# A gated-recurrence block and a bilinear FFN on one core: the output tile split by rows, and a unit's DMAs scheduled one by one

## The chip, the cores and the metric

The kernel runs on one core of a Trainium2 chip. The metric is the time of the whole program on the device, in microseconds: the median of several runs. Beside it there is one profiled execution, whose own time and span are given with the profile.

The core's engines run their own instruction lists in order and wait for each other on semaphores. They are named as in the profile: PE is TensorE (PEld its weight loads), DVE is VectorE, ACT is ScalarE, POOL is GpSimd, SP is SyncE, which does nothing here but put DMA transfers in (SPq in the rows). An instruction that must wait holds up all that is behind it on its engine.

## What is computed

```python
# attention: B, H, S, D = 4, 8, 768, 48
f = 1.0 / (1.0 + np.exp(-f_logit))
for t in range(S):
    state = f[:, :, t, :, None] * state + np.einsum('bhd,bhe->bhde', k[:, :, t], v[:, :, t])
    y[:, :, t] = np.einsum('bhd,bhde->bhe', q[:, :, t], state)
# bridge: (B, H, S, D) -> x of (B*S, H*D) = 3072 x 384
a = x @ w_a            # 384 x 1536
b = x @ w_b            # 384 x 1536
out = (a * b) @ w_out  # 1536 x 384
```

Everything is float32; the results have 3072 rows of 384.

## The kernel before

**Tiles and stages.** The 3072 tokens are cut into 8 blocks of 384 (half a sequence of one batch entry). A block's attention is done in two *units* of four heads each, 16 units in all. A unit is loaded into one of three sets of tiles (`NSET = 3`; `q`, `k`, `f`, `v`), so the loads of unit u + 3 can only follow when unit u is done.

A unit passes through these steps. The *front* (`front_parts`, L281): ScalarE makes two sigmoids of f (`opposite`, L294, and `sigmoid`, L291), GpSimd one affine step (L297), VectorE the running products (L301, L304, L309, L314), and multiplies q and k by them (L318). The *core* (`core_parts`, L845): TensorE makes scores of k and q (L364), VectorE masks them (L387), TensorE turns k (transposes, L399), ScalarE copies it out as `kT` (L409), TensorE forms the chunks' contributions to the state (`gains`, L423), VectorE adds them up (`carry`, L444 and L446, and `hand_on`, L455), TensorE forms y from the scores (`within`, L466) and from the state (`across`, L487), ScalarE copies y out of PSUM into `y_sb` (L512, three parts), and `stored` (L514) sends y into the block's `xT` by five DMAs (L531) and then issues the loads of unit u + 3: two of f, two of k and two of q (L215) and one of v (L217). `y_sb` has one buffer.

The FFN of a block is an *up*-projection (a, b and their product) and a *down*-projection. The first two blocks' ups are plain (`up`, L567). From the third block on the up is done with fewer products on sums of the operands (`combine_x`, L653, makes the sums with VectorE at L673; `up_triples`, L683, with matmuls at L689, copies by ScalarE and adds by VectorE, recorded at L1180 and L681). The down-projection takes token groups in pairs (`down`, L764, matmuls at L782), again with sums (L681). Each pair fills one tile `o` of 128 x 2 x 384, of which there is one buffer: row half 1 by `second` (ScalarE, L804), `sum_u3` (L813) and `last_of` (L816), row half 0 by `third` (ScalarE, L807) and `last_of`. `store(1)` and then `store(0)` send the halves out (SyncE, L820). `begin` copies one partial result to `u2` (L797).

**The order.** Startup, the weight conversions and the first four units are written out by hand. The rest is made by a list scheduler at build time. The list `main` holds the FFN's steps of the remaining blocks in order; each TensorE step is a *beat* of 656 ns. Every other step names its engine, an assumed load in ns and a `due`: the number of beats after which TensorE needs it. Beside `main` there are side lines (`Line`): sums of weights, sums of x, the core steps of the units, their fronts. `earliest` (L1099) gives the time at which a line's next step could start: the ends of the steps that it needs plus `LATENCY` (200 ns). `fill` (L1149) puts side steps in before each main step: a TensorE step when its inputs are ready by plan, another engine's step when its start is within a beat and `delays` (L1109) does not find that a due step of `main` on that engine would come late by it. `emit_until` (L1141) forces a line's steps in where main comes to need them (`beside`, `marks`).

In this plan the whole of `stored`, five stores and seven loads, is one SyncE step with a load of 0 ns, whose end is set 5000 ns after its start; the front of unit u + 3 needs that end. The output stores are SyncE steps of `main` with a load of 0 ns and no due.

Of the kernel before, what the change touches and what calls it, by code (L numbers as in the profile page):

```python
# [4 lines left out]

# [6 lines left out]
FP32 = mybir.dt.float32  # L12
# [9 lines left out]
BLK = 384  # L22
# [110 lines left out]
def by_quotients(ctx, tc, q, k, f_logit, v, moe_w_a, moe_w_b, moe_w_out, out, ident, weights, bad):  # L133
# [57 lines left out]
    def unit(u):  # L191
        b, r = divmod(u, NH * NQ)
        return (b, *divmod(r, NQ))

    def load_unit(u, names="fkqv"):
        if u >= NU:
            return
        b, half, qd = unit(u)
        t = sets[u % NSET]
        cols = slice(half * BLK, half * BLK + BLK)  # L200
        if u - NSET in FIRST and "f" in names:
            nc.gpsimd.memset(t["f"], 30.0)
        for nm, src in (("f", f_logit), ("k", k), ("q", q)):
            if nm not in names:
                continue
            if nm == "f" and u in FIRST:

                for par in range(2):
                    row = ((b * H + 4 * qd + par) * D) * S + half * BLK
                    rows = bass.AP(src.tensor, src.offset + row, [[S, R], [2 * D * S, 2], [1, BLK]])  # L210
                    nc.sync.dma_start(out=t[nm][R * par:R * par + R], in_=rows)
                continue
            heads = src[b].rearrange("(n two) d s -> two d n s", two=2)
            for par in range(2):
                nc.sync.dma_start(out=t[nm][R * par:R * par + D], in_=heads[par][:, 2 * qd:2 * qd + 2, cols])  # L215
        if "v" in names:
            nc.sync.dma_start(  # L217
                out=t["v"].rearrange("s n c x -> s n (c x)"),
                in_=v[b, 2 * qd:2 * qd + 2, :, half * NC:half * NC + NC].rearrange("n s c two d -> s n (c two d)"),
            )  # L220
# [293 lines left out]
    def stored(u):  # L514

        b, half, qd = unit(u)
        give_back(live[u].pop("y"))
        y = live[u].pop("y_sb").rearrange("r (n c) p m -> r n (c p m)", n=2)

        blk = b * NH + half  # L520
        if qd == 0:
            xT[blk] = sb2.tile([128, NKT, BLK], FP32, tag="xT", name="xT")
        for n in range(2):
            for h in range(2):
                ch, row, left = (4 * qd + 2 * n + h) * D, R * h, D
                while left:
                    kt, p = divmod(ch, 128)
                    w = min(left, 128 - p)

                    queue = nc.scalar if u < NQ and (n + h) % 2 else nc.sync  # L530
                    queue.dma_start(out=xT[blk][p:p + w, kt], in_=y[row:row + w, n])  # L531
                    ch, row, left = ch + w, row + w, left - w
        live.pop(u - NQ, None)
        if u >= NQ:
            load_unit(u + NSET)

# [5 lines left out]

    BEAT = 4 * 164
    beats = [0]

# [218 lines left out]
    def down(pair):  # L764
# [34 lines left out]
        def part(i, j):  # L799
            return got["o"][:, i, HM * j:HM * j + HM]  # L800

        def second():
            got["o"] = sb1.tile([128, 2, DM], FP32, tag="o", name="o")
            nc.scalar.copy(part(1, 0), m1)  # L804

        def third():
            nc.scalar.copy(part(0, 0), x0)  # L807

# [9 lines left out]
        def store(i):  # L818
            blk, g = pair[i]
            nc.sync.dma_start(out=out[blk * BLK + g * 128:blk * BLK + g * 128 + 128], in_=got["o"][:, i])  # L820

# [17 lines left out]
        yield on(DVE, 270, 8, last_of, 1, 0, x1)  # L839
        yield on(SP, 0, 0, store, 1)  # L840
        yield from times(m0, s4, b22)
        yield on(DVE, 270, 4, last_of, 0, 1, m0)
        yield on(SP, 0, 0, store, 0)

    def core_parts(s):  # L845
# [24 lines left out]
        if u >= 2 * NQ:  # L870
            for part in range(3):
                yield ACT, 490, 0, out_of_bank, u, part
            yield SP, 0, 5000, stored, u

# [33 lines left out]
    with tc.manual_schedule():  # L908
# [157 lines left out]

        for_out, for_x, core, fore, for_ba = lines = [Line() for _ in range(5)]
        marks = {"out": for_out.extend(w_out_sums)}
# [3 lines left out]
        for s in range(2 * NQ, NU + 1):  # L1072
            if s < NU:
                loaded = (stores[s - NSET],) if s - NSET in stores else ()
                ready = fore.extend(
                    [(e, load, 0, *do) for part in front_parts(s) for e, load, *do in part], needs=loaded
                )
            for step in core_parts(s):
# [5 lines left out]
                )  # L1084
                if step[3] is stored:
                    stores[s - 1] = core, len(core.steps)
            if s > 2 * NQ and s % NQ == 0:
# [21 lines left out]
        def delays(engine, start, load):  # L1109
# [11 lines left out]
            for ready, cost, due in later:  # L1121
                if ready >= with_it:
                    return False
                with_it, without = (max(x, ready) + cost for x in (with_it, without))
                if with_it + 2 * LATENCY > max(starts.get(due, 1 << 30), without + 2 * LATENCY):
                    return True
# [22 lines left out]
        def fill():  # L1149
            more = True  # L1150
            while more:
                more = False
                for line in lines:
# [4 lines left out]
                    if engine == PE:  # L1158
                        fits = start <= now
                    else:  # L1160
# [371 lines left out]
```

## Time and profile before

| what | value |
|---|---|
| median of 3 runs | 612.3 us (611.85 to 612.41) |
| the profiled execution's own time | 612.89 us |
| its span, first to last instruction | 610.6 us |
| mean granted TensorE clock | 0.977 |
| last matmul ends, last add on VectorE starts | about 604.3 us |

The stages of the span, in microseconds from its start:

| stage | from | to |
|---|---|---|
| startup, weight loads and conversions, plain ups | 0 | 126 |
| list scheduler begins; last plain ups, units 4 and 5 | 126 | 150 |
| three down pairs (with units 4, 5, 6 beside them) | 150 | 207 |
| first up with sums (third block) | 207 | 257 |
| one down pair, then ups and downs by turns, fronts and cores of later units beside them | 257 | 480 |
| ups and downs with no attention left | 480 | 604 |

Some more groups of the page, in their own columns: line, engine, operation, names, shape and count; then busy us and mean ns of one; then the idle time just before them and what ended most of it.

```profile
L689 PE MATMUL ps_f<-xT,w_ba 128*128 128x192 f32 x384 | 78.6, 327 | 0.8 <-ACT groups L1180 0.8
L782 PE MATMUL ps_f<-w_out,sums 128*128 128x192 f32 x288 | 51.6, 327 | 0.0
L297 POOL TENSOR_SCALAR inv<-inv 128x768 f32<-128x768 f32 x14 | 12.3, 881 | 258.4 <-ACT inv L294 258.3
...
out_dram<-o SPq DMA_DIRECT2D x24, 192.0 KB, 2.3
f_in<-in_f_logit_dram SPq DMA_DIRECT2D x28, 144.0 KB, 3.1
xT<-y SPq DMA_DIRECT2D x46, 72.0 KB, 2.2
```

The last three lines are DMA issues: what goes where, how many, KB of each, and the median us from issue to landing. How to read the rows: idle time before a group counts only on the engine that sets the end; on the others it is time in which they had nothing to do. A wait is put down to the event that came last before it ended, which need not be the one that was waited for.

### The profile page before, as it was taken

The page shows a single profiled execution, that of the slowest core. Times are in us where ns is not written, and L with a number is a line of the kernel's source. Part 1 is how long each engine was busy: PE and PEld are TensorE (multiplying, and loading weights), DVE is VectorE, ACT ScalarE, POOL GpSimd, SP SyncE. Part 2 cuts the span into 40 slices and gives each one's busy share as a digit, 9 for nine tenths or more (in the row PEclk, how much of TensorE's full clock was granted, in tenths as well). Part 3 has the DMA queues.
Part 4 walks back from the last instruction along what each step waited for, and adds up shares of the span by engine and source line. Part 5 has one row for each costly group of instructions (what it writes and reads, how often), then busy time and mean ns, then how long its engine had stood idle before and what let it go on. Part 6 is the DMA issues. An engine that isn't in the chain of part 4 may idle for free.

```text
span 610.6 us, 13870 instructions
## 1 busy us (share of the span) xinstructions
PE 572.2 (94%) x5778; PEld 512.7 (84%) x5778; DVE 409.4 (67%) x762; ACT 269.9 (44%) x508; POOL 75.1 (12%) x69
## 2 busy tenths in 40 slices
PE   0759899999989999999999999999999999999995
PEld 0625555556989989899999999999999999999995
DVE  6768434578978768968877875768576255836741
ACT  6567498962321554326532344335431245235300
POOL 6333164544200000000000100000000000000000
PEclk9859999999998999999999999999999999999998
DMA  8878586139855134044002600041001100000000
GB/s 221 251 204 232 143 259 206 53 66 163 154 125 124 47 84 93 2 103 119 1 3 74 149 27 1 2 109 36 1 3 47 46 0 1 1 27 0 2 28 31
DMA packets 33336, 49.42 MB, mean 81 GB/s; under 512 B 3952, under 2 KB 25072, under 8 KB 33264
## 3 DMA queue, kind: packets, MB, share of 16 engines
q1 hardware_dynamic: 29984, 42.38, 25.8%
q0 software_dynamic: 2992, 5.77, 5.6%
q8 instruction: 47, 0.77, 0.6%
q10 hardware_dynamic: 288, 0.30, 0.2%
q14 instruction: 25, 0.20, 0.1%
HBM read 33.23 MB, written 4.72 MB: 62 GB/s over the span
## 4 chain that ended last, share of the span: by engine, by line
PE 85%; DMA 6%; DVE 3%; ACT 2%; issue 2%; SPq 1%; ACTq 0%; DVEq 0%
PE ps_f L689 36%; PE ps_f L782 26%; PE ps_f L567 15%; DMA xT<-y 2%; PE ps_y L487 2%; PE ps_y L466 1%; PE ps_x L423 1%; PE ps_x L364 1%; DMA f_in<-in_f_logit_dram 1%; PE ps_x L399 1%; DMA k_in<-in_k_dram 1%; DVE sums L681 1%; DMA out_dram<-o 1%; SPq L215 1%; DMA q_in<-in_q_dram 1%
## 5 line engine op out<-in xcount | busy, mean ns | idle before, releaser
L567 PE MATMUL ps_f<-xT,w_ba 128*128 128x384 f32 x288 | 100.1, 506 | 6.9 <-DMA xT<-y 3.7
L567 PEld LDWEIGHTS ps_f<-xT,w_ba 128*128 128x128 f32 x288 | 55.1, 195 | 47.2 <-issue 7.4
L1180 ACT COPY groups<-ps_f 128x384 f32<-128x384 f32 x120 | 57.7, 481 | 66.6 <-PE ps_f L689 43.0
L1180 ACT COPY sums<-ps_f 128x384 f32<-128x384 f32 x120 | 57.6, 480 | 64.0 <-PE ps_f L689 56.6
L689 PE MATMUL ps_f<-xT,w_ba 128*128 128x192 f32 x384 | 78.6, 327 | 0.8 <-ACT groups L1180 0.8
L689 PEld LDWEIGHTS ps_f<-xT,w_ba 128*128 128x128 f32 x384 | 64.7, 190 | 1.5 <-ACT groups L1180 1.1
L689 PE MATMUL ps_f<-groups,w_ba 128*128 128x192 f32 x288 | 55.2, 327 | 0.0
L689 PE MATMUL ps_f<-x_sums,raw 128*128 128x192 f32 x288 | 53.8, 330 | 0.4 <-ACT sums L1180 0.2
L782 PE MATMUL ps_f<-spare,sums 128*128 128x192 f32 x288 | 51.7, 332 | 0.0
L782 PE MATMUL ps_f<-w_out,sums 128*128 128x192 f32 x288 | 51.6, 327 | 0.0
L782 PE MATMUL ps_f<-w_out,groups 128*128 128x192 f32 x288 | 51.2, 328 | 0.0
L689 PEld LDWEIGHTS ps_f<-x_sums,raw 128*128 128x128 f32 x288 | 47.1, 190 | 2.8 <-ACT sums L1180 1.7
L689 PEld LDWEIGHTS ps_f<-groups,w_ba 128*128 128x128 f32 x288 | 48.0, 190 | 0.4 <-ACT groups L1180 0.2
L782 PEld LDWEIGHTS ps_f<-spare,sums 128*128 128x128 f32 x288 | 47.4, 192 | 0.5
L782 PEld LDWEIGHTS ps_f<-w_out,groups 128*128 128x128 f32 x288 | 47.2, 190 | 0.6
L782 PEld LDWEIGHTS ps_f<-w_out,sums 128*128 128x128 f32 x288 | 47.2, 190 | 0.3
L59 POOL TENSOR_SCALAR sums<-sums 128x768 f32<-128x768 f32 (+1 forms) x20 | 40.4, 2019 | 51.4 <-ACT sums L57 51.4
L681 DVE TENSOR_TENSOR sums<-sums,groups 128x768 f32<-128x768 f32 x36 | 34.4, 955 | 14.8 <-ACT groups L1180 14.4
L297 POOL TENSOR_SCALAR inv<-inv 128x768 f32<-128x768 f32 x14 | 12.3, 881 | 258.4 <-ACT inv L294 258.3
L681 DVE TENSOR_TENSOR sums<-ps_f,sums 128x384 f32<-128x384 f32 x60 | 32.9, 554 | 13.9 <-PE ps_f L689 12.5
L689 PE MATMUL ps_f<-x_sums,w_ba 128*128 128x192 f32 x192 | 39.3, 327 | 0.2 <-DVE sums L681 0.2
L689 PE MATMUL ps_f<-xT,raw 128*128 128x192 f32 x192 | 39.3, 327 | 0.0
(123 smaller groups left out, 857.2 us busy)
## 6 DMA issues: line engine op xcount, KB each, us to landing
raw<-w_ba POOLq DMA_DIRECT2D x11, 512.0 KB, 8.2
q_in<-in_q_dram SPq DMA_DIRECT2D x32, 144.0 KB, 4.0
k_in<-in_k_dram SPq DMA_DIRECT2D x32, 144.0 KB, 3.5
v_in<-in_v_dram SPq DMA_DIRECT2D x16, 288.0 KB, 4.4
raw<-in_moe_w_out_dram SPq DMA_DIRECT2D x6, 768.0 KB, 4.2
out_dram<-o SPq DMA_DIRECT2D x24, 192.0 KB, 2.3
f_in<-in_f_logit_dram SPq DMA_DIRECT2D x28, 144.0 KB, 3.1
xT<-y SPq DMA_DIRECT2D x46, 72.0 KB, 2.2
```

The costliest lines, as they stand in the source:

```text
L59: nc.gpsimd.tensor_scalar(h, h, HI_MAX, None, ALU.min)
L215: nc.sync.dma_start(out=t[nm][R * par:R * par + D], in_=heads[par][:, 2 * qd:2 * qd + 2, cols])
L297: nc.gpsimd.tensor_scalar(inv, inv, EXP_K, 1.0, ALU.mult, ALU.add)
L364: nc.tensor.matmul(ps[h][SUB * p:SUB * p + SUB, o:o + SUB], lhsT=kf[r, tokens(n, c, p)], rhs=qf[r, tokens(n, c, p)], start=True, stop=True,)
L399: nc.tensor.transpose(ps[n][:, c * C:c * C + C], kf[:, o:o + C], ident)
L423: nc.tensor.matmul(ps_x[R * h:R * h + D, p, (n * NC + c) * D:(n * NC + c) * D + D], lhsT=kT[r, n, c, R * h:R * h + D], rhs=t["v"][r, n, c, ...
L487: nc.tensor.matmul(ps[p][e:e + D, o:o + SUB], lhsT=st[j][r, n], rhs=qf[r, tokens(n, c, p)], start=False, stop=True, skip_group_check=True,)
L567: nc.tensor.matmul(ps[nm][:, 0:BLK], lhsT=w[:, kt, ft * 128:ft * 128 + 128], rhs=xT[blk][:, kt], start=kt == 0, stop=kt == NKT - 1,)
L681: nc.vector.tensor_tensor(to, x, y, op)
L689: nc.tensor.matmul(ps[:, g], lhsT=sums_of_w[name][:, g, 128 * j:128 * j + 128], rhs=sums_of_x[blk][name], start=start and g == 0, stop=Tru ...
L782: nc.tensor.matmul(to, lhsT=x[:, i // 2, i % 2], rhs=w[:, NI * (i % 2) + i // 2], start=start and i == 0, stop=i == HFT - 1, skip_group_ch ...
L1180: do(*args)
```

## The change

It has three parts.

The output tile `o` becomes two tiles of 128 x 384, `o1` and `o0`, each with one buffer. `second` takes the first, `third` the other; `store(1)` reads the first and `store(0)` the other.

The DMAs of a unit become steps of their own for the list scheduler. `stores_of(u)` yields the bookkeeping (`begin`) and then each store of y, `loads_of(u)` each load. `core_parts` gives every store to the scheduler as a SyncE step of 430 ns (`ISSUE`) whose end is set 5000 ns behind it. A new side line, `loads`, holds the seven loads of the unit that takes the place of a stored one: each a SyncE step of 430 ns with an end 6000 ns behind it; the first needs the end of the last store, and the front of that unit needs the last load. The output stores become steps of 430 ns that are due after 3 beats, so that `delays` takes them into account. In the part written out by hand `stored` and `load_unit` run the same stores and loads in the same order as before.

The margins: `delays` allows 500 ns where it allowed 400 (`2 * LATENCY`), and a side step on TensorE is put in when its start by plan plus 200 ns (`LATENCY`) is not after the present, where it was its start alone.

```diff
     def load_unit(u, names="fkqv"):
+        for do in loads_of(u, names):
+            do()
+
+    def loads_of(u, names="fkqv"):
...
+        def load(to, src):
+            nc.sync.dma_start(out=to, in_=src)
...
             for par in range(2):
-                nc.sync.dma_start(out=t[nm][R * par:R * par + D], in_=heads[par][:, 2 * qd:2 * qd + 2, cols])
+                yield partial(load, t[nm][R * par:R * par + D], heads[par][:, 2 * qd:2 * qd + 2, cols])
...
     def stored(u):
 
+        for do in stores_of(u):
+            do()
+        if u >= NQ:
+            load_unit(u + NSET)
+
+    def stores_of(u):
+
         b, half, qd = unit(u)
-        give_back(live[u].pop("y"))
-        y = live[u].pop("y_sb").rearrange("r (n c) p m -> r n (c p m)", n=2)
-
         blk = b * NH + half
-        if qd == 0:
-            xT[blk] = sb2.tile([128, NKT, BLK], FP32, tag="xT", name="xT")
+
+        def begin():
+            give_back(live[u].pop("y"))
+            if qd == 0:
+                xT[blk] = sb2.tile([128, NKT, BLK], FP32, tag="xT", name="xT")
+            live.pop(u - NQ, None)
+
+        def store(n, h, kt, p, row, w):
+            y = live[u]["y_sb"].rearrange("r (n c) p m -> r n (c p m)", n=2)
+            queue = nc.scalar if u < NQ and (n + h) % 2 else nc.sync
+            queue.dma_start(out=xT[blk][p:p + w, kt], in_=y[row:row + w, n])
+
+        yield begin
         for n in range(2):
             for h in range(2):
                 ch, row, left = (4 * qd + 2 * n + h) * D, R * h, D
                 while left:
                     kt, p = divmod(ch, 128)
                     w = min(left, 128 - p)
-
-                    queue = nc.scalar if u < NQ and (n + h) % 2 else nc.sync
-                    queue.dma_start(out=xT[blk][p:p + w, kt], in_=y[row:row + w, n])
+                    yield partial(store, n, h, kt, p, row, w)
                     ch, row, left = ch + w, row + w, left - w
-        live.pop(u - NQ, None)
-        if u >= NQ:
-            load_unit(u + NSET)
...
     BEAT = 4 * 164
+    ISSUE = 430
...
         def part(i, j):
-            return got["o"][:, i, HM * j:HM * j + HM]
+            return got["o", i][:, HM * j:HM * j + HM]
 
         def second():
-            got["o"] = sb1.tile([128, 2, DM], FP32, tag="o", name="o")
+            got["o", 1] = sb1.tile([128, DM], FP32, tag="o1", name="o1")
             nc.scalar.copy(part(1, 0), m1)
 
         def third():
+            got["o", 0] = sb1.tile([128, DM], FP32, tag="o0", name="o0")
             nc.scalar.copy(part(0, 0), x0)
...
         yield on(DVE, 270, 8, last_of, 1, 0, x1)
-        yield on(SP, 0, 0, store, 1)
+        yield on(SP, ISSUE, 3, store, 1)
         yield from times(m0, s4, b22)
         yield on(DVE, 270, 4, last_of, 0, 1, m0)
-        yield on(SP, 0, 0, store, 0)
+        yield on(SP, ISSUE, 3, store, 0)
...
-            yield SP, 0, 5000, stored, u
+            begin, *stores = stores_of(u)
+            yield SP, 0, 0, begin
+            for do in stores:
+                yield SP, ISSUE, 5000, do
...
-        for_out, for_x, core, fore, for_ba = lines = [Line() for _ in range(5)]
+        for_out, for_x, core, fore, loads, for_ba = lines = [Line() for _ in range(6)]
...
-                loaded = (stores[s - NSET],) if s - NSET in stores else ()
+                loaded = ()
+                if s - NSET in stores:
+                    at = stores[s - NSET]
+                    loaded = (loads.extend([(SP, ISSUE, 6000, do) for do in loads_of(s)], needs=(at,)),)
...
-                if step[3] is stored:
-                    stores[s - 1] = core, len(core.steps)
+            if s > 2 * NQ:
+                stores[s - 1] = core, len(core.steps)
...
-                if with_it + 2 * LATENCY > max(starts.get(due, 1 << 30), without + 2 * LATENCY):
+                if with_it + 500 > max(starts.get(due, 1 << 30), without + 500):
...
-                        fits = start <= now
+                        fits = start + LATENCY <= now
```

## The prediction

> **What bounds the kernel now.** I read the page's first two parts first, to see which engine fills the span and where it does not.
>
> ```profile
> span 610.6 us, 13870 instructions
> PE 572.2 (94%) x5778; PEld 512.7 (84%) x5778; DVE 409.4 (67%) x762; ACT 269.9 (44%) x508; POOL 75.1 (12%) x69
> ...
> PE   0759899999989999999999999999999999999995
> ...
> PEclk9859999999998999999999999999999999999998
> ```
>
> TensorE sets the time: 572.2 of 610.6 us, and after the first six slices it is full but for slices 12 and 13. So only what makes TensorE wait, or slows its clock, can move the end. The profiled execution took 612.89 us, 2.3 us more than its span; the median of the runs is 612.3, so its stalls are taken as those of the runs and subtracted from 612.3.
>
> Next the windows of 15 us, for TensorE's missing time and its clock. Up to about 126 us (the last weight conversions) the order is written out by hand, and the change issues the same things in the same order there. From 315 to 600 us TensorE is busy 285.00 of 285.00 us: nothing can be won there. Between them stand the rows that matter (columns: length, then busy time of PE, PEld, DVE, ACT, POOL with counts, clock, DMA share, GB/s):
>
> ```profile
> 165.00:180.00 15.00, 14.67 (x178) 14.06 (x176) 12.51 (x23) 1.42 (x4) 0.00 (x0) 1.00 0.54 127
> 180.00:195.00 15.00, 13.16 (x142) 13.09 (x143) 11.97 (x29) 3.53 (x9) 0.83 (x1) 0.89 0.52 124
> ...
> 210.00:225.00 15.00, 14.18 (x261) 13.32 (x260) 9.37 (x16) 7.10 (x15) 0.83 (x1) 1.00 0.44 101
> 225.00:240.00 15.00, 14.96 (x90) 14.00 (x89) 13.69 (x28) 8.41 (x19) 0.00 (x0) 1.00 0.45 99
> 240.00:255.00 15.00, 14.57 (x174) 13.29 (x173) 12.87 (x25) 7.75 (x15) 0.83 (x1) 1.00 0.01 2
> ...
> 285.00:300.00 15.00, 14.10 (x173) 13.26 (x172) 11.88 (x18) 8.22 (x17) 0.83 (x1) 1.00 0.29 68
> 300.00:315.00 15.00, 14.82 (x92) 14.53 (x91) 11.84 (x19) 7.08 (x17) 0.00 (x0) 1.00 0.01 1
> ```
>
> The missing time is 0.33 + 1.84 = 2.17 us around 180, 0.82 us in 210 to 225, and 0.04 + 0.43 + 0.90 + 0.18 = 1.55 us after it: 4.54 us in all. The clock of 0.89 in 180 to 195 costs more: a finer window, 183.2 to 186.6, shows 0.50, so 3.4 us of matmuls did 1.7 us of work. The most that the change can win is thus 4.54 + 1.7 = 6.2 us, one per cent.
>
> Then the timeline, for what ended those waits. The first, in order of time (SPq is SyncE issuing a DMA):
>
> ```profile
> 167.27 0.37 SPq L820 DMA_DIRECT2D out_dram<-o  x1
> 167.73 3.04 SPq L531 DMA_DIRECT2D xT<-y  x5
> ...
> 173.83 0.42 SPq L217 DMA_DIRECT2D v_in<-in_v_dram  x1
> 174.34 0.42 SPq L820 DMA_DIRECT2D out_dram<-o  x1
> ...
> 178.90 0.32 ACT L804 COPY o<-ps_f 128x192 f32<-128x192 f32 x1 [8.43 <-DMA out_dram<-o]
> ...
> 180.99 0.80 ACT L409 COPY kT<-ps_x 128x768 f32<-128x768 f32 x1
> ...
> 181.84 0.70 PE L423 MATMUL ps_x<-v_in,kT 64*48 64x48 f32 x38 [2.16 <-ACT kT L409]
> ```
>
> The second output half of the pair was summed by 168.56 (its add on VectorE starts at 168.20 and takes 0.36), but its store stands in SyncE's order behind five stores and seven loads of an attention unit and goes out at 174.34. The next pair writes into the same single buffer `o`; ScalarE therefore stood 8.43 us, and behind it stood the copy of kT that TensorE needs. Its transposes were done at about 178.4, so kT could have been there before 179.7, where TensorE ran dry.
>
> The second wait: ScalarE's L294 for the front of unit 9 starts at 216.86 after 3.87 us idle. The view names an add on VectorE that does not write its inputs; the second load of f_in was issued at 213.8 and such loads land after 2.8 to 3.6 us, which is 216.6 to 217.4. So this is a front put before its data had come; L1180 behind it was late and TensorE lost 0.82 us.
>
> **The output tile as two.** No instruction is added or removed: 24 stores of 192 KB, 24 copies and 48 adds of `o` stay. `second` now waits for store 1 of the pair before (issued 167.27, landing 1.8 to 4.8 us later, so by 172.1) and would be ready at about 172.1 (its matmuls run from 169.95 to 171.9). `third` waits for store 0, and is ready at about 174.0; with the store out at 168.6 it lands by 170.4 to 173.4. What stands behind `second` on ScalarE is L294, `third`, L291 and the kT copy at L409; TensorE waits for the last. All 2.17 us go if store 0 is not held up; if it is, `third` waits instead and the copy behind it with it. The two waits of ScalarE on that tile are 12.3 us; the other one, 3.9 us ending at 195.89, costs TensorE nothing (15.00 of 15.00 us busy from 195 to 210) and I count it at nothing.
>
> The slow clock followed at 183.2, that is 3.5 us after TensorE ran dry at 179.7, and TensorE was at full speed in every other window from 60 to 600 us, with waits of up to 0.9 us from 185 on. So I put it down to this gap and take all 1.7 us; from below the bound is 0. The Trainium skill, "TensorE: Matmul & The Clock Gate", section "HAM oscillation — how this bites in real kernels", speaks against that: by it only idle gaps of more than about 3.4 us matter, and 2.17 us would not drop the clock. By that rule the sum would be 1.7 us smaller, 609.3; the row shows the drop after the shorter gap, and I go by the row.
>
> **DMAs one by one, loads behind the stores.** The 5 stores and 7 loads of a unit remain 12 issues on SyncE, 3.04 us and about 3.2 us in the timeline. Now each is a step of 430 ns, an output store can go between them, and the loads follow only when the last store is 5.2 us past by plan. For unit 4 (y copied out by 164.9) stores end by plan at about 167.3 and loads start at 172.5: store 0 of the pair (168.6) is ahead of them. The front of the unit three later is planned 5 x 0.43 + 5.2 + 7 x 0.43 + 6.2 = 16.6 us after the first store, where it was 5.2. The real way is 3.4 us of stores, 1.8 us for the two f_in issues and 3.0 us of landing, 8.2 us: the old plan was too early and the new one is not. The 0.82 us of the second wait go; bounds 0 to 0.82, and I take 0.82 because nothing else in ScalarE's queue was late there.
>
> Cost of the delay of 11.4 us per unit: unit 7 was stored from 227.4, and the sums of its block (L673) start at 257.1, after the up-projection before them has ended; 239 would still be 18 us ahead of them. Unit 5, the tight one, was stored at 184.3, its sums ran from 193.5 to 199.1 and their use began at 207.3, 8.2 us of cover; its stores come earlier by up to 2.6 us (kT at 178.4 instead of 181.0), and the plan pays 2.2 us more for five issues. Hence nothing. Without that cover each us late would be a us of TensorE.
>
> **Wider margins.** Side work on VectorE and ScalarE is refused 100 ns sooner, and a side step on TensorE is put in 200 ns after its inputs' planned end. The steps stay the same; each may slip by a beat (0.65 us), hidden by the same slack. This is aimed at such waits as the 0.90 us at 293.9 (transposes for a mask not yet done) and four of about 0.2 us. No row shows how the new order falls out. Bounds: it wins all 1.55 us, or adds as much again. I take 0, the middle, since VectorE is 13.69 of 15 us busy at 225 to 240, where any new order is as exposed as the old.
>
> **Sum.** 2.17 + 1.7 + 0.82 + 0 = 4.7 us; 612.3 - 4.7 = 607.6. All terms at their best give 606.1; without the second wait and with 1.55 us added, 2.17 + 1.7 - 1.55 = 2.3 gives 610.0.
>
> **Rivals.** (a) Only the first stall goes, the second stays and the new order adds small ones of 1.55 us: 610.0 by the sum above. For it: such waits come from plans that differ from the chip by a few hundred ns, and 100 ns more margin is less than the 0.9 us seen. Against: the front no longer meets its loads.
>
> (b) A ScalarE queue blocked elsewhere takes the place of the first: fronts wait for k_in on VectorE six times, 9.8 us in all, up to 3.5 us, with TensorE's copies behind them. One gap like the first, with its slow clock, is 3.9 us: 607.6 + 3.9 = 611.5, no measurable change. Against: none of those six reached TensorE with more than 0.9 us.
>
> (c) Slower: the fronts, now 10 us later, pile up on VectorE in the first up-projection in threes (207 to 257). A front is 2 x 0.95 + 0.15 + 0.17 + 6 x 0.43 + 2 x 0.95 = 6.7 us of VectorE. The front of unit 9 moves from 217 to about 227 and would meet that of unit 10 (240 to 257) where VectorE has only 1.31 + 2.13 = 3.4 us free in 225 to 255. If it is put in all the same, 6.7 - 3.4 = 3.3 us of adds come late and TensorE waits as long, and the front of the next unit does it again: two such waits, each with the clock at half for 1.7 us, are 10 us, 607.6 + 10 = 617.6. It decides when new stalls exceed 4.7 + 1.2 = 5.9 us. Against: work that would make a due add late is refused by plan, more so than before, and unit 7 has 18 us of cover.
>
> **How the numbers follow.** A measurement of this kernel can tell 0.2%, 1.2 us, from no change. Chances: the forecast 0.62, (a) 0.12, (b) 0.10, (c) 0.16. Faster is the first two, 0.74; same is (b), 0.10; slower is (c), 0.16. The forecast's own range is 606.0 to 609.5. The range that should hold 8 in 10 runs from 605.7 (all terms at best, and 0.4 us for the two lengths of wait that I could not see) to 612.8, past (a) and (b), and leaves out most of (c).
>
> **What would show it.** Right: ScalarE's wait for the landing of `out_dram<-o` is gone from its waits; the output store of 174.34 stands ahead of the unit's loads; the clock is 1.00 in every window from 75 to 600; TensorE's missing time from 165 to 315 falls from 4.5 to under 2 us; the f_in load is issued well before L294 asks for it. Wrong: a new wait of over 1 us of TensorE in 165 to 350, on VectorE for (c), on ScalarE for (b); or a clock of half without a gap, which would take the 1.7 us out of the sum. A change of the time before 126 us or after 600 us would mean that something else than these steps moved it.

## The result, and the profile after

The changed kernel takes 611.91 us (median of 12 runs, 611.11 to 612.98), the kernel before 612.04 us (12 runs). The ratio is 0.9995, its 95% interval 0.9984 to 1.0007: no change that can be measured. The line numbers below are those of the changed kernel: matmuls of the plain ups L588, of the ups with sums L710, of the downs L803; adds L702; copies L1208; the front L301 to L328; `second` L825, `third` L829; kT L419; output stores L842.

The page of the changed kernel, its span and the granted clock in 40 slices:

```profile
span 611.1 us, 13867 instructions
...
PEclk9859999999999999999999999999999999999998
```

The slice of slow clock near 185 us is gone, as forecast, yet the span is not shorter. The windows of 15 us show where the time went (length, then busy time of PE, PEld, DVE, ACT, POOL with counts, clock, DMA share, GB/s):

```profile
165.00:180.00 15.00, 15.00 (x237) 14.61 (x227) 12.97 (x26) 2.74 (x7) 0.00 (x0) 1.00 0.51 134
180.00:195.00 15.00, 15.00 (x165) 14.70 (x164) 11.06 (x25) 4.70 (x10) 0.83 (x1) 1.00 0.47 119
...
210.00:225.00 15.00, 15.00 (x205) 14.49 (x197) 12.64 (x26) 6.50 (x14) 0.00 (x0) 1.00 0.46 101
225.00:240.00 15.00, 14.71 (x180) 14.06 (x179) 11.01 (x24) 9.15 (x20) 0.83 (x1) 1.00 0.13 36
240.00:255.00 15.00, 14.42 (x174) 13.83 (x173) 14.79 (x24) 5.93 (x14) 0.83 (x1) 1.00 0.35 67
255.00:285.00 30.00, 29.79 (x422) 28.47 (x421) 21.35 (x49) 12.90 (x28) 0.83 (x1) 1.00 0.25 69
285.00:300.00 15.00, 14.79 (x91) 14.48 (x90) 12.90 (x23) 7.46 (x15) 0.00 (x0) 1.00 0.38 90
300.00:315.00 15.00, 13.80 (x180) 11.97 (x181) 13.07 (x24) 6.83 (x15) 0.83 (x1) 1.00 0.01 1
315.00:600.00 285.00, 283.16 (x2550) 276.29 (x2543) 179.72 (x320) 99.79 (x220) 2.50 (x3) 1.00 0.11 30
```

The same long window of the kernel before:

```profile
315.00:600.00 285.00, 285.00 (x2573) 280.05 (x2572) 180.25 (x323) 101.82 (x222) 2.50 (x3) 1.00 0.11 30
```

The two early waits are gone (15.00 of 15.00 us from 165 to 225). But from 225 on TensorE misses time in every row, and 1.84 us in the long window where it had missed none.

A wait costs more than its idle time: some of the matmuls after it are slower too, by about 0.1 us each (at 370.05 us of the changed kernel, right after a wait, the next one starts 0.27 us later; the usual distance there is 0.16). So I went through TensorE's list, matmul by matmul, took the distance from one start to the next, less the usual distance between two matmuls of these two kinds (the median), and summed what exceeded it by over 0.05 us, stage by stage. The expectations quoted below count only pauses of over 0.11 us, which gives smaller numbers (1.85 for 2.90, 1.17 for 2.05). "Scheduled" is the time from the second matmul that the list scheduler placed (near 129 us) to the end of the last one; it leaves out the startup, which varies (last section). All in us:

| stage | before | after |
|---|---|---|
| three downs, 150 to 207 before | 4.98 | 0.66 |
| up of block 2 | 3.58 | 2.39 |
| up of block 3 | 2.36 | 3.79 |
| up of block 4 | 0.29 | 2.90 |
| up of block 5 | 0.51 | 2.05 |
| all else | 3.06 | 2.77 |
| sum | 14.78 | 14.56 |
| scheduled | 474.95 | 474.74 |

The changed kernel wins 4.3 + 1.2 + 0.3 = 5.8 us and loses 1.4 + 2.6 + 1.5 = 5.6 us. The table accounts for the whole difference (14.78 - 14.56 = 0.22, 474.95 - 474.74 = 0.21).

What is won, in the timeline of the changed kernel (start, duration, engine, line, what, idle time before it):

```profile
167.18 2.35 SPq L842 DMA_DIRECT2D out_dram<-o  x2
169.62 3.04 SPq L545 DMA_DIRECT2D xT<-y  x5
172.64 0.32 ACT L825 COPY o<-ps_f 128x192 f32<-128x192 f32 x1 [1.63 <-PE ps_f L803]
174.59 0.32 ACT L829 COPY o<-ps_f 128x192 f32<-128x192 f32 x1 [1.63 <-DVE w_ba L1167]
179.64 0.80 ACT L419 COPY kT<-ps_x 128x768 f32<-128x768 f32 x1 [4.73 <-DVE o L835]
181.44 0.70 PE L433 MATMUL ps_x<-v_in,kT 64*48 64x48 f32 x38
184.47 0.94 ACT L304 ACTIVATE inv<-f_in,less 128x768 f32<-128x768 f32 x1
```

Both output stores go out before the unit's stores, and ScalarE waits for TensorE and not for a landing (for L829 and L419 the view names work on VectorE that they do not read; the matmuls that they read ended at 174.55 and 179.56). TensorE takes kT without idle time. But note the last row: the front of unit 7 (L304) now stands behind the copy of kT, where it stood ahead of it before (179.11 against 180.99). That turns out to matter.

What is lost, at the worst place in the up of block 4:

```profile
368.38 0.47 DVE L324 TENSOR_TENSOR_SCAN inv<-inv,start,zero 128x128 f32<-128x128 f32 x1
368.77 0.40 DVE L324 TENSOR_TENSOR_SCAN inv<-inv,zero 128x128 f32<-128x128 f32 x1
369.08 0.46 DVE L324 TENSOR_TENSOR_SCAN inv<-inv,start,zero 128x128 f32<-128x128 f32 x1
369.46 1.00 DVE L702 TENSOR_TENSOR groups<-ps_f,groups 128x384 f32<-128x384 f32 x2
370.05 2.22 PE L710 MATMUL ps_f<-x_sums,raw 128*128 128x192 f32 x12 [0.90 <-DVE groups L702]
```

VectorE works on the front of unit 14 (L324), the two adds that free TensorE's PSUM banks (the memory that the matmuls write) come after it, and TensorE stands 0.90 us. The same place in the kernel before:

```profile
356.31 0.95 DVE L318 TENSOR_TENSOR k_in<-k_in,inv 128x768 f32<-128x768 f32 x1
370.61 1.14 DVE L681 TENSOR_TENSOR groups<-ps_f,groups 128x384 f32<-128x384 f32 x2 [0.54 <-PE ps_f L689]
371.64 2.11 PE L689 MATMUL ps_f<-x_sums,raw 128*128 128x192 f32 x12
```

There the front's last step (L318) was long done, and VectorE waited for TensorE. In the kernel before this front began at 347.2 (its L294), in the down-projection ahead, and ended at 357.3, 4 us into this up; now it runs from 358.6 to 376.7, deep inside it. That of unit 15 ran from 409.2 to 421.6, to 10 us into the up of block 5, and now from 418.1 to 436.0, to 27 us into it.

### The profile page after: what moved, and what is told of

Read it like the earlier page. It is cut to its first block, busy times and chain, and to the rows that moved or that the text cites. A ratio compares the mean times of both kernels' runs of the same rounds, so it can differ in the third digit from the quotient of the medians.

```text
span 611.1 us, 13867 instructions
## 1 busy us (share of the span) xinstructions
PE 572.6 (94%) x5778; PEld 511.6 (84%) x5778; DVE 410.5 (67%) x762; ACT 268.7 (44%) x508; POOL 76.1 (12%) x69
## 4 chain that ended last, share of the span: by engine, by line
PE 82%; DVE 5%; DMA 5%; ACT 2%; issue 2%; SPq 1%; ACTq 0%; DVEq 0%
PE ps_f L710 32%; PE ps_f L803 27%; PE ps_f L588 15%; DMA xT<-y 2%; PE ps_y L476 2%; PE ps_y L497 2%; PE ps_x L433 2%; PE ps_x L374 1%; DVE groups L702 1%; PE ps_x L409 1%; DMA f_in<-in_f_logit_dram 1%; DVE sums L702 1%; DMA k_in<-in_k_dram 1%; DVE inv L324 1%; DVE f_in L311 1%
## 5 line engine op out<-in xcount | busy, mean ns | idle before, releaser
L588 PE MATMUL ps_f<-xT,w_ba 128*128 128x384 f32 x288 | 99.6, 505 | 7.0 <-DMA xT<-y 3.7
L588 PEld LDWEIGHTS ps_f<-xT,w_ba 128*128 128x128 f32 x288 | 55.1, 195 | 47.0 <-issue 7.4
L1208 ACT COPY sums<-ps_f 128x384 f32<-128x384 f32 x120 | 57.6, 481 | 75.3 <-PE ps_f L710 68.7
L1208 ACT COPY groups<-ps_f 128x384 f32<-128x384 f32 x120 | 57.7, 481 | 68.4 <-PE ps_f L710 47.8
L710 PE MATMUL ps_f<-xT,w_ba 128*128 128x192 f32 x384 | 78.5, 327 | 0.0
L710 PEld LDWEIGHTS ps_f<-xT,w_ba 128*128 128x128 f32 x384 | 64.7, 190 | 0.3
L710 PE MATMUL ps_f<-x_sums,raw 128*128 128x192 f32 x288 | 53.7, 330 | 2.6 <-DVE groups L702 2.0
L710 PE MATMUL ps_f<-groups,w_ba 128*128 128x192 f32 x288 | 55.6, 328 | 0.0
L710 PEld LDWEIGHTS ps_f<-x_sums,raw 128*128 128x128 f32 x288 | 47.0, 190 | 5.5 <-DVE groups L702 3.2
L803 PE MATMUL ps_f<-w_out,groups 128*128 128x192 f32 x288 | 51.6, 328 | 0.0
L803 PE MATMUL ps_f<-w_out,sums 128*128 128x192 f32 x288 | 51.5, 327 | 0.0
L803 PE MATMUL ps_f<-spare,sums 128*128 128x192 f32 x288 | 49.8, 327 | 0.0
L710 PEld LDWEIGHTS ps_f<-groups,w_ba 128*128 128x128 f32 x288 | 47.9, 190 | 0.8 <-ACT sums L1208 0.4
L803 PEld LDWEIGHTS ps_f<-w_out,groups 128*128 128x128 f32 x288 | 47.2, 190 | 0.6
L803 PEld LDWEIGHTS ps_f<-w_out,sums 128*128 128x128 f32 x288 | 47.4, 190 | 0.2
L702 DVE TENSOR_TENSOR sums<-sums,groups 128x768 f32<-128x768 f32 x36 | 35.3, 980 | 18.0 <-ACT groups L1208 17.6
L803 PEld LDWEIGHTS ps_f<-spare,sums 128*128 128x128 f32 x288 | 47.0, 190 | 0.1
L702 DVE TENSOR_TENSOR sums<-ps_f,sums 128x384 f32<-128x384 f32 x60 | 33.0, 553 | 20.0 <-PE ps_f L710 16.2
L710 PE MATMUL ps_f<-x_sums,w_ba 128*128 128x192 f32 x192 | 39.6, 329 | 1.0 <-DVE groups L702 0.5
L710 PE MATMUL ps_f<-xT,raw 128*128 128x192 f32 x192 | 39.8, 330 | 0.2 <-ACT groups L1208 0.2
```

The costliest lines, as they stand in the source:

```text
L588: nc.tensor.matmul(ps[nm][:, 0:BLK], lhsT=w[:, kt, ft * 128:ft * 128 + 128], rhs=xT[blk][:, kt], start=kt == 0, stop=kt == NKT - 1,)
L702: nc.vector.tensor_tensor(to, x, y, op)
L710: nc.tensor.matmul(ps[:, g], lhsT=sums_of_w[name][:, g, 128 * j:128 * j + 128], rhs=sums_of_x[blk][name], start=start and g == 0, stop=Tru ...
L803: nc.tensor.matmul(to, lhsT=x[:, i // 2, i % 2], rhs=w[:, NI * (i % 2) + i // 2], start=start and i == 0, stop=i == HFT - 1, skip_group_ch ...
L1208: do(*args)
```

## The experiments

Two theories of the give-back: **A**, the planned ends of the new DMA steps (16.6 us from a unit's first store to the front three units later, where it was 5.2) push the fronts into the ups with sums; **B**, something else does, the margins above all. Ratios are to runs of the kernel before on the same chip, with 95% intervals.

| experiment | ratio | interval | scheduled | downs to 207 | up 2 | up 3 | up 4 | up 5 |
|---|---|---|---|---|---|---|---|---|
| before | 1 | | 474.95 | 4.98 | 3.58 | 2.36 | 0.29 | 0.51 |
| after | 0.9995 | 0.9984 to 1.0007 | 474.74 | 0.66 | 2.39 | 3.79 | 2.90 | 2.05 |
| tile only | 0.9972 | 0.9947 to 0.9998 | 471.55 | 2.19 | 3.02 | 2.36 | 0.29 | 0.51 |
| old margins | 1.0006 | 0.9980 to 1.0032 | 474.92 | 1.09 | 2.86 | 1.80 | 2.89 | 2.05 |
| margins only | 0.9966 | 0.9944 to 0.9988 | 473.27 | 1.64 | 5.87 | 1.47 | 0.29 | 0.98 |
| one tile | 0.9987 | 0.9965 to 1.0009 | 474.46 | 0.66 | 2.39 | 3.79 | 2.63 | 2.04 |
| fronts held | 0.9948 | 0.9929 to 0.9967 | 472.44 | 0.66 | 2.38 | 3.79 | 0.46 | 0.74 |
| real loads | 0.9924 | 0.9902 to 0.9947 | 471.54 | 1.09 | 4.20 | 1.46 | 0.59 | 1.24 |
| one step, real end | 0.9938 | 0.9913 to 0.9962 | 471.84 | 0.83 | 1.69 | 3.51 | 0.53 | 0.74 |
| plan's wait alone | 0.9983 | 0.9960 to 1.0005 | 473.38 | 1.18 | 2.92 | 1.80 | 1.27 | 1.89 |
| slower issues | 0.9950 | 0.9933 to 0.9967 | 472.08 | 0.83 | 2.14 | 2.55 | 1.32 | 2.59 |
| tile and margins | 0.9965 | 0.9948 to 0.9983 | 474.01 | 1.93 | 6.31 | 1.47 | 0.29 | 0.98 |

### Old margins: are they the cause?

The changed kernel with these two lines as before:

```diff
-                if with_it + 500 > max(starts.get(due, 1 << 30), without + 500):
+                if with_it + 2 * LATENCY > max(starts.get(due, 1 << 30), without + 2 * LATENCY):
...
-                        fits = start + LATENCY <= now
+                        fits = start <= now
```

> The changed kernel with the old margins (400 ns, and TensorE's side steps without the 200 ns). Theory A (what the change wins early it gives back because the loads' planned ends put the fronts of later units 11 us later, into the ups with sums): the fronts of units 14 and 15 stay in the ups of blocks 4 and 5, as the plan has them, and the new waits of about 3.7 us there stay: 611.2 to 612.6 us. Rival B (the wider margins moved the side work): these waits go and the early gain is kept: about 608.0 us.

The run took 611.89 us. The ups of blocks 4 and 5 lose 2.89 and 2.05 us, as in the changed kernel (2.90 and 2.05). The margins are not what gives the gain back there; with the other two parts of the change in place they are worth 474.92 - 474.74 = 0.2 us. That is a sum of larger parts: without them the up of block 3 loses 1.80 us instead of 3.79, but the down-projection before it 1.58 instead of 0.33, and the first downs and the up of block 2 lose 0.43 and 0.47 us more.

### Margins only

The same two lines changed in the kernel before, and nothing else.

> The kernel before with the wider margins alone; one output tile, a unit's DMAs in one step. Theory A: ScalarE still stands for the landing of the output half near 179 and the clock drops after it, so the early 3.9 us are not won; the fronts of units 14 and 15 stay where they were and the ups of blocks 4 and 5 have no new waits: 611 to 612.5 us. Rival B (margins cause the give-back): the early loss stays and about 4 us of new waits come to it: about 616 us.

609.65 us. The ups of blocks 4 and 5 keep their pace (0.29 and 0.98), so theory B fails a second time. But my expectation failed too: the early wait is gone, without the tile or the new DMA steps. The wider margins changed the order of SyncE's work, so that both output stores go out ahead of the unit's DMAs (L807 is `third`, and it waits for TensorE):

```profile
164.05 2.35 SPq L820 DMA_DIRECT2D out_dram<-o  x2
166.50 3.04 SPq L531 DMA_DIRECT2D xT<-y  x5
171.47 0.32 ACT L807 COPY o<-ps_f 128x192 f32<-128x192 f32 x1 [1.63 <-PE ps_f L782]
```

The up of block 2 pays for part of it with 5.87 us: the fronts there now come before their f_in data, and ScalarE waits for such loads for 8.7 us in all between 165 and 225.

### Tile only

The kernel before with `o1` and `o0` and nothing else.

```diff
...
-            got["o"] = sb1.tile([128, 2, DM], FP32, tag="o", name="o")
+            got["o", 1] = sb1.tile([128, DM], FP32, tag="o1", name="o1")
...
+            got["o", 0] = sb1.tile([128, DM], FP32, tag="o0", name="o0")
...
```

> The kernel before with the output tile split in two and nothing else: SyncE's order of DMAs and all margins stay. Theory A (the queue holds the stall, the tile alone frees little): the store of row half 0 still goes out behind five stores and seven loads at about 174.3 and lands at about 178.9; now `third` waits for it instead of `second`, and L294 and `second` get ahead. The copy of kT stands behind `third`, so TensorE's gap near 181 shrinks by at most 1 us and the clock still drops: 611 to 612 us. Rival B (the single tile is the cause, its split is enough): the gap of 2.17 us and the slow clock of 1.7 us go: 608.1 us.

611.43 us, ratio 0.9972. The median lies in A's range, but the interval is wide (0.1 to 3.2 us won); in the profile the scheduled part is 3.4 us shorter, more than A says and less than B. The timeline of this kernel (L808 is `third`):

```profile
174.07 0.94 ACT L294 ACTIVATE inv<-f_in,less 128x768 f32<-128x768 f32 x1 [2.18 <-DMA f_in<-in_f_logit_dram]
...
178.23 0.32 ACT L808 COPY o<-ps_f 128x192 f32<-128x192 f32 x1 [3.13 <-DMA out_dram<-o]
178.44 0.85 ACT L291 ACTIVATE f_in<-f_in 128x768 f32<-128x768 f32 x1
179.19 0.79 ACT L409 COPY kT<-ps_x 128x768 f32<-128x768 f32 x1
...
180.03 0.70 PE L423 MATMUL ps_x<-v_in,kT 64*48 64x48 f32 x38 [0.89 <-ACT kT L409]
```

The mechanism is A's: the landing is now waited for by `third`, with the kT copy behind it. But L294 has already run, and the copy comes at 179.19 instead of 180.99 (1.16 us earlier in the scheduled part, which began 0.64 us earlier here); TensorE's gap is 0.89 instead of 2.16 us, and the clock stays at full speed. So in the three downs the split alone wins 2.8 of the 4.3 us: a gap shorter by 1.27 us, and no slow clock after it.

### One tile

The changed kernel with the single tile `o`.

```diff
...
-            got["o", 1] = sb1.tile([128, DM], FP32, tag="o1", name="o1")
+            got["o"] = sb1.tile([128, 2, DM], FP32, tag="o", name="o")
...
-            got["o", 0] = sb1.tile([128, DM], FP32, tag="o0", name="o0")
...
```

> The changed kernel with the single output tile of before; DMAs one by one and the margins as changed. Theory A (order of the queue is what counts): the store of half 0 goes out at about 169.2, before the loads, and lands before `second` of the next pair is ready at about 172, so no wait comes back: 611.2 to 612.6 us, as the changed kernel. Rival B (the split of the tile is needed): the wait for the landing returns with its gap and its slow clock, 3.9 us: about 615.8 us.

611.53 us, and the same table within 0.3 us: theory A. Once the output stores go out ahead of the unit's DMAs, the split of the tile changes nothing.

### Fronts held: is it the fronts' place?

The changed kernel, with the fronts of units 14 and 15 held until the ups of blocks 4 and 5 are through:

```diff
-                    [(e, load, 0, *do) for part in front_parts(s) for e, load, *do in part], needs=loaded
+                    [(e, load, 0, *do) for part in front_parts(s) for e, load, *do in part], needs=loaded,
+                    past={14: behind[4], 15: behind[5]}.get(s, 0),
```

> The changed kernel with one more rule for the scheduler: the front of unit 14 is not put in before the up of block 4 is through, that of unit 15 not before the up of block 5. In the changed kernel both lie in these ups, where the matmuls lost 1.85 and 1.17 us against their usual pace; in the kernel before these ups lost 0.14 and nothing. Theory A (the fronts there are what gives the gain back): both losses go, nothing comes instead, since the downs that follow have VectorE idle and unit 15 is needed only at about 537 us: 3.0 us less in the scheduled part, about 608.9 us. Rival B (the losses come from the order of DMAs or of TensorE's side steps): they stay, 611.9 us. Rival C: they move with the fronts into the down-projections: 611 to 612 us.

609.51 us, ratio 0.9948. This is the decisive run: the two ups go from 2.90 and 2.05 to 0.46 and 0.74 us. Up to 404 us, past the end of the up of block 4, every engine's order is that of the changed kernel but for the front of unit 14. In the up of block 5 the core steps that need the front of unit 15 are gone too; around them, near 437 us, the changed kernel lost 0.2 us. TensorE's waits from 345 to 460 us in the changed kernel (what waited, on what; us in total, times, longest):

```profile
PE ps_f L710 <- DVE groups L702: 1.6, 3, 0.9
PE ps_f L710 <- ACT groups L1208: 0.2, 1, 0.2
```

and in this one:

```profile
PE ps_f L803 <- DVE u L832: 0.5, 1, 0.5
```

The waits on the ups' adds are gone; one of 0.5 us has come in a down. With that one the later downs and the up of block 6 lose 1.5 us more than in the changed kernel, so a part of C held too: of 3.75 us, 2.3 stay won in the scheduled part.

### Plan's wait alone: the other way round

The kernel before, with an empty step of 11.2 us in the plan between a unit's DMAs and the front three units later. The chip gets the same instructions, in another order:

```diff
...
-                loaded = (stores[s - NSET],) if s - NSET in stores else ()
+                loaded = ()
+                if s - NSET in stores:
+                    loaded = (landed.extend([(SP, 0, 11200, lambda: None)], needs=(stores[s - NSET],)),)
```

> The kernel before, where by plan alone a front may start 11.2 us later after the stores (an empty step in the scheduler, no instruction on the chip); output tile, order of DMAs and margins as before. Theory A (the planned wait alone makes the new losses): the fronts of units 14 and 15 fall into the ups of blocks 4 and 5 as in the changed kernel, which then lose 2 to 3.5 us, while the wait for the output half near 179 stays as it was: 614 to 616 us. Rival B (the planned wait is harmless): 612.0 us.

611.23 us, no measurable change. Half of the expectation held: the ups of blocks 4 and 5 lose 1.27 and 1.89 us instead of 0.29 and 0.51, with the old tile, the old order of DMAs and the old margins. The other half did not, and this corrects the prediction. ScalarE's timeline (L804 is `second`, L807 `third`, L409 the kT copy, L294 the front of unit 7):

```profile
178.87 0.32 ACT L804 COPY o<-ps_f 128x192 f32<-128x192 f32 x1 [7.96 <-PE ps_x L399]
179.09 0.33 ACT L807 COPY o<-ps_f 128x192 f32<-128x192 f32 x1
179.30 0.82 ACT L409 COPY kT<-ps_x 128x768 f32<-128x768 f32 x1
...
183.19 0.94 ACT L294 ACTIVATE inv<-f_in,less 128x768 f32<-128x768 f32 x1
```

ScalarE still stands 7.96 us until 178.87. (The view names transposes that it does not read; the output store went out at 174.79 and landed 4.0 us later, by this trace.) Yet TensorE hardly loses anything, 1.18 us in all three downs, since the front of unit 7 is no longer between that wait and the kT copy: the copy starts at 179.30 instead of 180.99. The 2.17 us gap was the wait *and* the two sigmoids behind it, and the planned wait takes the second away.

### Real loads

The changed kernel with the plan's ends nearer to what the traces show.

```diff
-                yield SP, ISSUE, 5000, do
+                yield SP, ISSUE, 5000 if do is stores[-1] else 0, do
...
-                    loaded = (loads.extend([(SP, ISSUE, 6000, do) for do in loads_of(s)], needs=(at,)),)
-                ready = fore.extend(
-                    [(e, load, 0, *do) for part in front_parts(s) for e, load, *do in part], needs=loaded
+                    loaded = (loads.extend([(SP, ISSUE, 3200, do) for do in loads_of(s)], needs=((at[0], at[1] - 1),)),)
+                parts = front_parts(s)
+                fore.extend(
+                    [(e, load, 0, *do) for part in parts[:-1] for e, load, *do in part],
+                    needs=tuple((of, n - 5) for of, n in loaded),
                 )
+                ready = fore.extend([(e, load, 0, *do) for e, load, *do in parts[-1]], needs=loaded)
```

> The changed kernel with shorter planned times: the loads follow the last store's issue instead of its planned landing, a load ends 3.2 us after its issue by plan (the traces show about 3.0 for f_in), and the front needs only the two f_in loads, its last part the others. By plan a front may start 6.6 us after the first store instead of 16.6. Theory A (the long planned ends are the cause): the front of unit 14 moves ahead by 12 us, mostly out of the up of block 4; 1 to 2.5 us of the 3.0 lost in the ups of blocks 4 and 5 come back: 609.4 to 610.9 us. Rival B (the planned ends don't matter): 611.9 us.

608.48 us, ratio 0.9924, the lowest ratio of all here, 3 to 6 us below the kernel before by its interval, and below the range of theory A: besides 3.1 us in the ups of blocks 4 and 5, 2.3 us in that of block 3 come back. The front of unit 14 runs from 345.3 to 358.2, the up of block 4 loses 0.59 and that of block 3 1.46 instead of 3.79 us. The up of block 2 loses more, 4.20:

```profile
210.26 0.94 ACT L304 ACTIVATE inv<-f_in,less 128x768 f32<-128x768 f32 x1 [3.42 <-DMA f_in<-in_f_logit_dram]
...
212.07 0.46 ACT L1211 COPY sums<-ps_f 128x384 f32<-128x384 f32 x1
212.43 0.48 ACT L1211 COPY groups<-ps_f 128x384 f32<-128x384 f32 x1
...
212.96 0.92 PE L710 MATMUL ps_f<-groups,raw 128*128 128x192 f32 x4 [1.64 <-ACT groups L1211]
```

That is the second wait of the kernel before, come back larger: a front that the plan put in before its data had come. ScalarE stands 3.42 us, the copies (L1211) behind the front are late and TensorE stands 1.64 us.

### Slower issues

The kernel of the real loads with a store's issue at 620 ns, a load's at 500, and a load's end at 3600.

> The experiment with real loads, with three numbers of the plan set to what its trace showed: 620 ns for a store's issue instead of 430, 500 ns for a load's, and a load's end 3.6 us after it instead of 3.2. There ScalarE stood 3.4 us at 210 for an f_in load that the plan had landed, and the matmuls of the first up with sums lost 3.06 us, 1.6 of them at that place. Theory A (a front planned too early makes ScalarE stand, one planned too late falls into an up): the front of unit 9 moves some 8 us, ScalarE no longer stands for its load, the first up loses about 1.3 us as in the changed kernel: 1.5 us less, about 607 us. Rival B (any move of a front makes as much new waiting as it ends): no change from 608.5 us, or more.

609.18 us. At the place that it was aimed at theory A is right: the up of block 2 falls from 4.20 to 2.14 us, and the waits for f_in between 165 and 225 to 1.6 us in all. In the sum B is right: the ups of blocks 3, 4 and 5 lose 1.1, 0.7 and 1.4 us more. The fronts in them start within 0.8 us of where they did, but the ups start 4.3, 3.2 and 1.0 us earlier, so the fronts lie deeper in them. Whether the depth is all of it, or the order of a front's steps among an up's adds counts too, no run here sorts out.

### One step with a real end

The kernel before with the tile split, the margins, the two fronts held, and:

```diff
-            yield SP, 0, 5000, stored, u
+            yield SP, 0, 8500, stored, u
```

> The kernel before (a unit's DMAs in one step) with the tile split, the wider margins, a planned end of 8.5 us after the stores instead of 5.0, and the fronts of units 14 and 15 held as in the experiment with held fronts. Tests whether the DMAs need to be steps of their own. Theory A (what was lost near 181 can be avoided without it, and the fronts' place decides the rest): 607.5 to 609.5 us. Rival B (without output stores going in between, a wait for their landing costs TensorE 3.9 us again somewhere): 611.5 to 613 us.

608.10 us, ratio 0.9938: in theory A's range and as fast as the best within the intervals, with a unit's DMAs in one step. To win the early stall, DMAs as steps of their own are not needed either; the run with the margins only had shown as much.

### Tile and margins

Both of these edits in the kernel before, and nothing else.

> The kernel before with the tile split and the wider margins, a unit's DMAs in one step as before. Each alone made the run about 2 us shorter (ratios 0.997). Theory A (both end the one stall near 181, which can be won only once; the fronts of units 14 and 15 stay out of the ups of blocks 4 and 5): no more than the larger of the two, 609 to 610.5 us, and no loss of over 0.3 us in these two ups. Rival B (they end different waits): the gains add, about 607.8 us.

610.35 us, ratio 0.9965. The gains of the two (0.9972 and 0.9966) do not add: they end the same stall, and the up of block 2 pays 6.31 us, much as with the margins alone. The ups of blocks 4 and 5 lose 0.14 us and nothing in pauses of over 0.11 us, as the expectation counts. Theory A.

## Why the prediction was wrong

It forecast 607.6 us and a gain of 4.7; measured is no change. By its own steps:

**The first stall, 2.17 + 1.7 us: right in size.** The three downs lose 0.66 instead of 4.98 us. The reason given was one of several. The change removes the stall more than once. The output stores no longer stand behind the loads; the one-tile run shows that this is enough, and either of two parts brings it about: the DMA steps with the old margins (output stores at 167.37 and 168.69, the loads from 171.55) or the wider margins alone (164.05, the unit's stores from 166.50). And the front of unit 7 no longer stands ahead of the kT copy; the run with the plan's wait alone shows that this is nearly enough too. The split of the tile, which the prediction put first, adds nothing once the output stores go first.

**The second wait, 0.82 us: right.** TensorE is busy 15.00 of 15.00 us from 210 to 225; the up of block 2 loses 1.2 us less.

**The margins, 0: right in the sum, and by luck**, 0.2 us by the run with the old margins: some 2 us won elsewhere and 2 us lost in the up of block 3. Alone they take 1.7 us off the scheduled part, by the same early stall.

**"Cost of the delay of 11.4 us per unit ... Hence nothing": this is the step that failed.** It asked only whether a unit would be late for its own use, found 18 and 8.2 us of cover, and priced the delay at nothing. No unit was late. But a front is 6.7 us of VectorE, and what it costs is set by where it falls: little around the start of an up with sums (0.29 and 0.51 us in the kernel before), some 0.8 us each in the downs and after (the fronts held), and 2 to 3 us deep inside an up, where adds that free TensorE's banks queue behind it. The ups of blocks 3, 4 and 5 lose 1.43, 2.61 and 1.54 us more, 5.6 us. The runs with the old margins, with the fronts held and with the plan's wait alone show this from three sides for blocks 4 and 5, where 4.15 of the 5.6 us were lost. All runs together show how the price grows with the depth. Where the front of unit 14 or 15 ended at most 10 us after the start of its up, that up lost 0.29 to 0.59 us; at 17 to 19 us 0.98 to 1.32; at 21 to 25 us 1.27 to 2.59; at 26 to 29 us 2.04 to 2.90.

For block 3 it is not shown. Two fronts lay in its up before and after, now 16 and 20 us deeper in it. In the run with the plan's wait alone they lie 9 and 13 us deeper than before, and the up lost less, 1.80 us; there the down-projection ahead of it lost 1.55 instead of 0.27, with 1.80 us of a front's scans (L301) directly before an add (L810) that TensorE waited 1.0 us for. The 3.79 us come with the DMA steps and the wider margins together: with the old margins the up lost 1.80, with the margins only 1.47. Why is open.

Rival (c) had this mechanism, fronts piling up on VectorE in an up with sums, but in the wrong place and at the wrong price. It looked at 207 to 257, where VectorE was fullest; there the loss fell. The new ones came from 284 to 435 us, most of them in ups that TensorE ran through almost without a pause before, since the fronts ended early in them. A full TensorE was read as "nothing can be won there"; it also meant that there was everything to lose. And (c) put it at 10 us, with the clock at half. The sum of the new losses was 5.6 us, just under the 5.9 from which it said that the kernel would be slower, and the clock never dropped.

So more than the expected gain was made, 5.8 us, and given back later. The planned ends of the DMA steps alone do much of both: they clear the way of the kT copy, and they push fronts into the ups.

## What to carry to other kernels

When a planner's estimate of a latency is changed, ask not only whether the work that waits for it can afford to be late, but in which stage it will land, and what is due there on the same engine. An estimate that is too short makes an engine stand for data with everything behind it; one that is too long moves work out of the stages that had room for it; take both ends from the trace. And a stall has as many causes as there are instructions between the late event and the one that the critical engine needs: moving any of them away may end it.

## What the runs showed of the hardware

**The clock after a gap.** TensorE was granted half its clock for 3.4 us after an idle gap of 2.16 us and 1.3 us of small matmuls, in the one profile of the kernel before. After gaps of 0.89 (tile only), 1.1 (old margins) and 1.64 us (real loads) it stayed at full speed. The Trainium skill, "TensorE: Matmul & The Clock Gate", section "HAM oscillation — how this bites in real kernels", puts the bound at gaps of about 3.4 us; the row of the kernel before shows a drop after a shorter one. Whether every run of that kernel has it is open, as the other runs have no trace.

**The startup varies by itself.** The part written out by hand has the same order in all kernels, and yet its first 128 us had different clocks. The kernel before:

```profile
0.00:128.00 128.00, 100.52 (x987) 62.19 (x988) 76.09 (x143) 91.38 (x133) 51.55 (x46) 0.92 0.67 187
```

and the one with the margins only:

```profile
0.00:128.00 128.00, 100.31 (x995) 62.53 (x996) 77.56 (x145) 93.89 (x136) 53.00 (x48) 0.96 0.64 187
```

By these means over 128 us (0.92 and 0.96) the clock was at half for 20.5 us of the first and 10.2 us of the second, and the scheduled part, as counted above, began at 129.0 and 126.5 us. Over all profiles that time lies between 126.5 and 129.7. Differences of this size in the spans of two profiles say nothing about the edit; that is why the tables compare the scheduled part.
